# Weights and half of the data transposed by DMA in a fused S4 and linear attention kernel

## The chip, the cores and the metric

The kernel runs on one core of a Trainium2 chip. A core has five engines that run their own instruction queues: TensorE (PE; matmuls and transposes, with weight loads counted apart as PEld), VectorE (DVE), ScalarE (ACT), GpSimd (POOL) and SyncE (SP), which in this kernel issues nearly all DMAs. The metric is the device time of one execution in microseconds (us), as the median over runs; lower is better.

## The reference

Two layers read the same input x (2048 tokens x 512 channels, bf16) and are mixed by a gate of each token. Cut to what matters:

```python
g = sigmoid((x * gate_w).sum(-1, keepdims=True))
# A: a state space convolution of each channel d
K = einsum("dn,dnl,dn->dl", C, exp(dt * A * l), dt * B).real       # 512 x 2048 filter
y = irfft(rfft(pad(x)) * rfft(pad(K)))[:2048] + x * Dskip
# B: linear attention, 32 heads of 16
q, k, v = split(x @ wqkv)
phi(t) = concat([softmax(t @ w_phi), softmax(-(t @ w_phi))])
o = phi(q) @ (phi(k).T @ v) / (phi(q) . sum(phi(k)) + 1e-6)
out = g * y + (1 - g) * (o @ wo)
```

## The kernel before

**A plan with an order of its own.** The kernel does not emit instructions as it is read. Its functions register steps in a list (Plan.add, line 106; a DMA is registered by Plan.dma, line 127, as an issue, a transfer and a landing). Each step has an engine, or a choice of two; the steps it needs; and the rings (PSUM banks, buffers) it takes and drops. Plan.run (line 148) emits the steps in the order of the table ORDER, two characters a step, each pair a number in base 64 that counts in the list. For steps with two engines the string SIDES says which; for steps with two PSUM rings RINGS does; WARM puts up to six dummy matmuls ahead of a step (line 1560), FOURS says for each of the 16 filter units whether a product is summed by TensorE (four terms) or ahead of it by DVE (step A3, lines 1111 to 1115, then two terms), and ZPS says for each of the 8 key pairs whether the sums of the softmax are formed by TensorE first (lines 718 to 725). The costs that steps carry served to make these tables and have no part in the emitted program. Every engine, SP too, works through its own steps strictly in that order.

**The stages**, by the timeline of the profile:

1. To about 26 us: tables of sines (ACT) and index patterns, loads, and transposes. SP issues the q and k weights (load_wqk, line 1506, one DMA of 1 MB into wqk), small constants, the parameters of A, the input in 16 DMAs (load_ud, line 1495, tile UD, tokens on partitions), the v weights (load_wv). TensorE transposes two things. The input: eight steps xps (lines 493 to 506) of eight 128x128 transposes each, evicted into xT (step xT, channels on partitions; 16 blocks j of 128 tokens). The weights: fold (line 512), once for k and once for q, does two steps wtp of 16 transposes, evicted by two steps wTe into wT, and then two steps wps that multiply wT with the block matrix Wphi made from w_phi; their evictions wpe write the folded weights (WW[0:4] for k, Wqp for q). So the product with w_phi is folded into the projection.
2. From 26 to about 96 us: the keys (attention_keys, line 655) and the spectrum of the input (lines 566 to 641). For each of 8 key pairs s2 there are two products pk of a block of xT with WW, their exponentials ek (ACT, tile Ek), the sums zk (DVE, line 731 or 734), their reciprocals rz (ACT), two products vp for the values, evicted as vb, scaled by DVE (vr), and products kn that add to kvp. Every pk of a pair's first block waits for all of xT and all of the folded key weights (line 713: `[sp] + xt + kp`). Between them, for two halves of the channels, copies UDp of the input (step udc), products psAu evicted as XAu, and products psBu evicted as xst (step XU), which go to DRAM (XUd, step xuw). DVE and ACT also make the filter tables (p_ steps).
3. From 96 to about 225 us: for 16 units of 32 channels, filter products on DVE (A1, A2, A3, Rh, Rl, El), their sum over states on TensorE (kps), and transforms of the filter (psA, XA; psB, XK; product with XUX, step t128; psz, Zr; transposed through DRAM or by DVE; psy; step ou); beside them queries and attention outputs (plan_queries, line 809).
4. The tail: the last two units alone, and stores.

All evictions of PSUM go through one helper (Plan.copy, line 142), so the profile shows them under line 144 (ACT) and line 146 (DVE); the tile's name tells them apart. Exponentials and sines are line 68. The steps pzw and pzr (lines 343 to 356) write two small products of the parameters to DRAM and read them back as statE and statC in 8 DMAs each; statC is needed by the first sines of the units (tile cs).

Of the kernel before, what the change touches and what calls it, by code (L numbers as in the profile page):

```python
# [70 lines left out]
class Plan:  # L71

    DIGITS = "0123456789abcdefghijklmnopqrstuvwxyzABCDEFGHIJKLMNOPQRSTUVWXYZ-_"
    ORDER = ("0B0C0D0H0I0J2P000K0L0M112R2t2v0S0U0_100V120W0P0y0z0A2y2u0N0T14150O0Q0Y0X0Z18172Q2S2w2x0405060s0t0u0d0e0f0708090g0h0i0102030j"
             "0k0l0a0b0c0m0n0o0p0q0r0v0w0x130R2T2V2U2W2X2Z2Y2J2K192-0-1a1c1u2H1w1l162I1F2_311x1m1y1n1d1G1H3330322z2A341v2B2F2D1b2C352E1e1A"
             "1C2G1z361D2N2L2O37392M1o1p1q0E0F0G1r1s1t1B1E1W3a1J384A4H4J4I4K4W4Y4X4Z4O4L3b3d4S4M4P3e4N4T4Q4U1N3c513f554R4V3h4-3g563i4_5052"
             "5357595a5b5c5d3j5g1O3k543l585k5l5o5p5h3m5e5f1K5i4B5q4C5m5r5s3P5t3n5v5z3p5j5n3o5w5A1I1Q5u5D5E5F5G5H3u1L3q5x5B3w3x5K5O5y5C5S5L"
             "4D3v5P1R3r3s3t3y3z3A5T5I3Q3R5J5M5Q5U5Z1S5V1X1T1U1P3B3D3E615N5W625X5Y3C5R5-4E635_653I673K1M66683J3L3S6064696k6m3T3V6l6n6o6c6a"
             "6p3W3U6b6q6d3X3Z3Y6r3_3-1V1Z1Y406e1-1_25216s206t6v41433M3N3O3F3G3H1f1g1h426g45444647492627484a4b4c4d4e4g284f4h6h2b6i292a2d2c"
             "224i4j4k4l4n4o2e2m2f232g242h6w2i2j2n4m2o6f6j2q2p2r2k4s4t4p4q4r1i1j1k2l2s4u4v4w4x4y4z6E6G8j6x8x8y6u8i8n8k8m8o8l6y8p8q4F8u6z4G"  # L80
             "8z6D8v8w8A8B6F6H6I8D8E8R6K7b8C8F8J8K8G8H8I6J6L6M8S7c6N7d7f7haf6O8X8T7e7g6P6Q8Yag7i8L7K8-7M6R6S6T6U9c9d9e6V6W6X6Z6-6_8M8_7j8N"
             "7O8P7L8O7k8Q7N8U8V94907l957m7n8W8Z7Pao7Qap7oa5a9aa919293ah6Y707p7q7r6A6B6C9f9g9h9i9j9k7s7t7u7w7x7y9697a6a87173abadalamaq74ai"
             "aj72akauav98759a99a79bacae7RanaC777SaD9o7T789p76aras7vaE7U7VataI7Wawax9waL7A7C9x9q9y7XaM7D9r9z9s9AaJc6c77zaFaG9EbY7E7G7FaN7Y"
             "7Z7-7_80818384858r8s8t9B9C9D9t9u9v9l9m9nb0b1b2c09Fc17BaRaHc882869GaSb-c39M9NayaA87azaBaKb_7H88898b7Ic4aOaPaQ9Occcd8abZ8c7J8d"
             "aTc2c5aUcfcg8e79aVaW8f7a8gaXc9cachcbclcm8h9H9PcCaY9IcD9Qcectb9cubadZaZa-a_b6b7b89R9S9T9J9K9Ld-bhbicicjcEbbckcIcJbjd_e0cncobc"
             "bkbdbleMe1bpbxeN9-cvczcwcxcAe2bqbye3e4cQcRcSb3b4b59U9V9W9X9Y9ZbebfbgcyeOe5cpcrcqcse69_eVeWbra0dQcBa1a2dPdTdVdUcFcGa3bzeXcHeS"
             "a4cKbscLbte7e8e9bmbnboeaebeceeefegcTcUcVbubvbwcMcNcOcPdRbAd0d8bBbCbDbEcZc-c_d1d9ePeQeRedeTehd2daeUeidgdWejdhd3dod4dpdbdSdcdX"
             "dYcWcXcYe_f0eYeZdie-dqbFbGbHbIbJbKd5d6d7eGeHeIdddedfeAeBeCbLbMdjf1flbNdrdkfmdsdldmdnfGbOf2fHekbPf3f5eldCfofpfnfrfqfMbQfsfIfN"
             "bRf4f6ftf7fafuf8fvfJfKfLdtdudveDeEeFdwdxdydzdAdBdDdFdGfbfwdHdIf9fcfxfOfyeJeKeLemfPfQfzfRfSfTdEenfAfdfgfefffUeqfhfVfWfXfYfifZ"
             "f-eoerf_esepg0g1g2fBfjfCfDg3fkg4bSbTbUbVbWbXdMdNdOdJdKdLetexeyezeuevewfEfFg5g6g7g8g9ga")  # L90
    SIDES = ("01110001001011111100111001000001010101110000001110000000000011101000101111111100010100010000000000000000000000000000"
             "0000000000000000000000000010000000000000000001100001001")
    RINGS = ("00101010111010010100000000000000000000001010000000000000011001000010000000100110111010100010011111101100101101001111"
             "00100001")
    WARM = ("00000000000000610000000000002000060000000000000040000010000030000000000500050203000040000041500000000000100020000000"
             "00000000000002000000000")
# [97 lines left out]
def prepare(P, nc, g, evict, psum):  # L194

    fc, act, persist, at = g.fc, g.act, g.persist, g.at
    F = Bag()
# [19 lines left out]
    P.dma("wqk", 0.5, 2.0, lambda: g.load_wqk(), rw=("", "wqk"), move=3.3)  # L217
# [294 lines left out]
def fold(P, nc, g, evict, psum, first, dst, name):  # L512

    F, fn, out = Bag(), [], []
    for h in range(2):
        box = Bag()

        def fa(h=h, box=box):
            if h == 0:
                F.wT = g.up.tile([128, 4, 512], BF16, name=name, tag="wT")  # L520
            box.ps = psum([128, 4, 512], "wtp", BF16)
            for mm in range(2):
                for kt in range(4):
                    c0 = first + 128 * (2 * h + mm)
                    nc.tensor.transpose(out=box.ps[:, mm, 128 * kt:128 * kt + 128], in_=g.wqk[:, kt, c0:c0 + 128], identity=g.ident[:])

        def fe(h=h, box=box):
            i = box.ps[:, 0:2]
            box.ps = None
            return F.wT[:, 2 * h:2 * h + 2, :], i  # L530
        a = P.add("PE", "wtp", fa, [a] if h else [], take=[("ps", "p0")] + ([] if h else ["wT"]), rw=("wqk ic", ""))
        fn.append(evict("wTe", fe, [a]))
    for h in range(2):
        box = Bag()

        def fb(h=h, box=box):
            box.ps = psum([128, 2, 512], "wps")
            for k in range(2):
                for m in range(4):
                    kt = 2 * h + k  # L540
                    nc.tensor.matmul(box.ps[:, k, 128 * m:128 * m + 128], lhsT=F.wT[:, m, 128 * kt:128 * kt + 128], rhs=g.at.Wphi[:, m, :],
                                     start=True, stop=True)
# [12 lines left out]
def keys_and_spectrum(P, nc, g, psum):
# [8 lines left out]
    polar, sx, xt, kp = prepare(P, nc, g, evict, psum)  # L564
# [864 lines left out]
def full_kernel(tc, A_u, A_A_re, A_A_im, A_B_re, A_B_im, A_C_re, A_C_im, A_log_dt, A_Dskip,  # L1429
# [7 lines left out]
    with ExitStack() as ctx:  # L1437
        g, fc, at = Bag(), Bag(), Bag()
        P = Plan(nc, {"XAu": 1, "UDp": 1, "xst": 2, "wT": 1, "Ek": 2, "Zk": 2, "vr": 2, "vb": 2, "acc": 1, "r8": 3, "ax": 1, "nrm": 1, "E": 2, "cs": 4, "A": 1, "R": 2,
                      "KD": 1, "XA0": 1, "XK": 2, "Zr": 2, "XUX": 3, "ln": 8}, {"ps": 2, "p0": 2, "bk": 3, "acc": 1, "pf": 2})  # L1440
# [190 lines left out]
```

## Time and profile before

| | |
|---|---|
| median of 3 runs | 252.65 us (252.41 to 253.89) |
| the profiled execution | 252.06 us, span 250.3 us |
| mean granted TensorE clock | 0.957 |
| busy: PE, PEld, DVE, ACT, POOL | 206.6, 141.3, 234.2, 221.2, 8.7 us |
| HBM read and written | 21.38 MB, 12.58 MB |

The profile comes from one execution. An engine's busy time is the union of its instructions; neighbours overlap by a little under 0.1 us, so the durations of single instructions add up to slightly more. In a row of a timeline stand start and length in us, engine, line of the code, operation, the tile written and the tiles read; SPq and ACTq are the DMA issues in the queues of those engines. The span runs from the first to the last instruction, the profiled time also holds what lies around it.

### The profile page before, as it was taken

What the parts mean: (1) busy time and instruction counts of PE and PEld (TensorE: products, weight loads), DVE (VectorE), ACT (ScalarE), POOL (GpSimd) and SP (SyncE); (2) the same over time, 40 slices, a digit from 0 to 9 for tenths busy, and PEclk for the clock granted to TensorE, in tenths of its full rate; (3) what the DMA queues carried; (4) which work ended last, traced back from release to release, by engine and by line L of the source; (5) the groups of instructions that cost most, each with busy time, mean ns of one, the idle gap of its engine ahead of it and who ended that gap; (6) DMA issues with size and microseconds to landing.
All of it is one profiled execution on the core that took longest, in us unless ns stands there. A gap on an engine that the chain in (4) does not pass through costs nothing. (4 is left out here: it accounts for less than half of the span.)

```text
span 250.3 us, 9879 instructions
## 1 busy us (share of the span) xinstructions
PE 206.6 (83%) x4393; PEld 141.3 (56%) x4415; DVE 234.2 (94%) x318; ACT 221.2 (88%) x305; POOL 8.7 (3%) x21
## 2 busy tenths in 40 slices
PE   0675999999984685999988887999989789889960
PEld 0675656555754432365656645775678467777530
DVE  7999998899999999999999999999999999998880
ACT  3998998999999999999999999999999997892830
POOL 5700000000000000000000000000000000000000
PEclk9999999999997596899999999999999999999996
DMA  7997000080551755003787049723595989872934
GB/s 187 220 218 182 18 3 4 3 243 14 145 151 59 198 150 146 3 3 115 182 245 185 5 122 204 245 86 66 157 245 133 237 230 319 197 226 50 220 75 84
DMA packets 52842, 34.86 MB, mean 139 GB/s; under 512 B 30528, under 2 KB 48320, under 8 KB 52800
## 3 DMA queue, kind: packets, MB, share of 16 engines
q1 hardware_dynamic: 51744, 33.98, 53.4%
q8 instruction: 34, 0.56, 0.9%
q10 hardware_dynamic: 1056, 0.26, 0.5%
q14 instruction: 8, 0.07, 0.1%
HBM read 21.38 MB, written 12.58 MB: 136 GB/s over the span
## 5 line engine op out<-in xcount | busy, mean ns | idle before, releaser
L178 PE MATMUL kps<-R,A 128*32 128x64 bf16 x1600 | 29.1, 229 | 2.5 <-ACT XK L144 0.8
L178 PEld LDWEIGHTS <-A 128*32 128x32 bf16 x1600 | 27.2, 160 | 6.5 <-issue 3.0
L68 ACT ACTIVATE cs<-args 128x1024 bf16<-128x1024 f32 x32 | 30.6, 1050 | 0.0
L1102 DVE TENSOR_TENSOR A<-Ctab,Dtab 128x2048 bf16<-128x2048 bf16 x16 | 19.5, 1218 | 0.6 <-PE kps L178 0.6
L1123 DVE TENSOR_TENSOR R<-E,cs 128x2048 bf16<-128x2048 bf16 x16 | 19.5, 1218 | 0.0
L1107 DVE TENSOR_TENSOR A<-Ctab,Dtab 128x2048 bf16<-128x2048 bf16 x16 | 19.5, 1218 | 0.0
L1119 DVE TENSOR_TENSOR R<-E,cs 128x2048 bf16<-128x2048 bf16 x16 | 19.5, 1217 | 0.0
L144 ACT CAST XA<-psA 128x1024 bf16<-128x1024 f32 (+1 forms) x17 | 16.1, 986 | 2.5 <-PE psA L185 2.4
L144 ACT CAST Zr<-psz 128x1024 bf16<-128x1024 f32 (+1 forms) x16 | 15.8, 1025 | 2.0 <-DMA Zd<-Zr 1.6
L68 ACT ACTIVATE Ek<-pk 128x512 bf16<-128x512 f32 x32 | 16.6, 611 | 1.0 <-PE pk L704 1.0
L68 ACT ACTIVATE E<-args 128x1024 bf16<-128x1024 f32 x16 | 16.8, 1052 | 0.4 <-issue 0.2
L68 ACT ACTIVATE Eq<-pq 128x512 bf16<-128x512 f32 (+1 forms) x28 | 16.8, 688 | 0.3 <-PE pq L838 0.3
L1233 DVE TENSOR_TENSOR t<-XUX,XK 128x2048 bf16<-128x2048 bf16 x14 | 16.9, 1219 | 0.1
L144 ACT CAST XK<-psB 128x1024 bf16<-128x1024 f32 (+1 forms) x17 | 16.1, 981 | 0.6 <-DVE t L1233 0.6
L838 PE MATMUL pq<-xT,Wqp 128*128 128x512 bf16 x64 | 16.5, 395 | 0.1
L752 PE MATMUL vp<-WW,xT 128*128 128x512 bf16 x62 | 15.7, 380 | 0.1
L704 PE MATMUL pk<-WW,xT 128*128 128x512 bf16 x57 | 14.8, 380 | 0.5 <-issue 0.2
L611 PE MATMUL psB<-XAu,TB 64*128 64x128 bf16 x256 | 11.0, 241 | 3.8 <-ACT xst L144 2.6
L731 DVE TENSOR_REDUCE Zk<-Ek 128x64 f32<-128x1024 bf16 x12 | 14.0, 1210 | 0.0
L65 ACT ACT_TABLE_LOAD x10 | 12.8, 1283 | 0.9 <-PEq L1615 0.7
L611 PEld LDWEIGHTS <-TB 64*128 64x128 bf16 x256 | 9.0, 106 | 8.0 <-issue 7.9
L761 DVE TENSOR_TENSOR vr<-vb,vr 128x1024 bf16<-128x1024 bf16 x16 | 10.5, 683 | 1.7 <-ACT vr L68 1.5
(213 smaller groups left out, 506.4 us busy)
## 6 DMA issues: line engine op xcount, KB each, us to landing
XUX<-XUd SPq DMA_DIRECT2D x32, 256.0 KB, 4.9
XUd<-xst SPq DMA_DIRECT2D x8, 512.0 KB, 3.0
ax<-apd SPq DMA_DIRECT2D x16, 256.0 KB, 5.1
Zd<-Zr SPq DMA_DIRECT2D x24, 128.0 KB, 3.5
ZT<-Zd SPq DMA_DIRECT2D x6, 512.0 KB, 6.1
UD<-in_A_u_dram SPq DMA_DIRECT2D x16, 128.0 KB, 4.2
XUd<-xst SPq DMA_DIRECT2D x8, 256.0 KB, 4.0
wqk<-in_B_wqkv_dram SPq DMA_DIRECT2D x1, 1024.0 KB, 5.5
```

Of the source, the lines that this page charges most:

```text
L68: return self.nc.scalar.activation(**kw)
L144: self.nc.scalar.copy(out=o, in_=i)
L178: nc.tensor.matmul(kps[32 * dj:32 * dj + 32, g4, e, :], lhsT=A[:, ka, :, :, d].rearrange("p a b -> p (a b)"), rhs=R[:, kr, d, :], start=(i ...
L611: nc.tensor.matmul(box.ps[:, c2, sl, :], lhsT=fc.TB[rows, b0:b0 + 2].rearrange("p a b -> p (a b)"), rhs=X.t[rows, k, r0 + sl].rearrange("p ...
L704: nc.tensor.matmul(box.ps[:], lhsT=xT[:, st, kt, :], rhs=g.WW[:, kt, :], start=(kt == 0), stop=(kt == 3))
L752: nc.tensor.matmul(box.ps[:], lhsT=xT[:, st, kt, :], rhs=g.WW[:, 4 + kt, :], start=(kt == 0), stop=(kt == 3))
L838: nc.tensor.matmul(box.ps[:, m - m0, :] if late else box.ps[:], lhsT=g.Wqp[:, kt, 128 * m:128 * m + 128], rhs=xT[:, 4 * b:4 * b + 4, kt, : ...
L1102: nc.vector.tensor_tensor(out=c.A[:, 0:2].rearrange("p o a b c -> p (o a) b c"), in0=g.C[U // 8][:, 0:2, :, d0 % 256:d0 % 256 + 32].rearra ...
L1107: nc.vector.tensor_tensor(out=c.A[:, 2:4].rearrange("p o a b c -> p (o a) b c"), in0=g.C[U // 8][:, 1:3, :, d0 % 256:d0 % 256 + 32].rearra ...
L1119: nc.vector.tensor_tensor(out=c.R[:, :, :, 32:64], in0=t.E[:, 1].unsqueeze(1).to_broadcast([128, 2, 32, 32]), in1=t.cs[:], op=ALU.mult)
L1123: nc.vector.tensor_tensor(out=c.R[:, :, :, 0:32], in0=t.E[:, 0].unsqueeze(1).to_broadcast([128, 2, 32, 32]), in1=t.cs[:, ::-1, :, ::-1], o ...
L1233: nc.vector.tensor_tensor(out=box.t, in0=Ls[r0 // ns].X[:], in1=box.XK[:].unsqueeze(1).to_broadcast([128, 2, 1024]), op=ALU.mult)
```

## The change

- The one load of the q and k weights becomes two DMA transposes of 512 x 512 (k first in the list, then q) straight into wqT, which has the layout that wT had. fold loses its wtp and wTe steps, and each wps waits for its own half.
- Of the eight xps steps, the last four (T8 = 4 to 7, token blocks j = 8 to 15) with their evictions are replaced: for each of the 8 blocks, four DMA transposes of 32 tokens x 512 channels from the input in DRAM into xT. The input itself is still loaded whole, as the spectrum needs it.
- The first pk of pair s2 waits for the rows of pair s2 alone.
- ORDER, SIDES, RINGS, WARM, FOURS and ZPS are new; the list has 1046 steps where it had 1035.

```diff
-    FOURS = ("0111110101011000")
-    ZPS = ("00000101")
+    FOURS = ("0111110001011000")
+    ZPS = ("00000001")
...
-    P.dma("wqk", 0.5, 2.0, lambda: g.load_wqk(), rw=("", "wqk"), move=3.3)
+    for k in (1, 0):
+        P.dma("wqT", 0.5, 2.0, lambda k=k: g.load_wqk(k), rw=("", f"wqT{k}"), move=2.6)
...
+        if T8 in g.TURN:
+            xt.append([P.dma("xtr", 1.6, 2.0, lambda j=2 * T8 + k: g.turn_x(j), move=1.0, cnt=4) for k in range(2)])
+            continue
         a = P.add("PE", "xps", tx, take=[("ps", "p0")], rw=(f"ud{T8 // 2} ic", ""))
-        xt.append(evict("xT", xe, [a]))
-    kp = fold(P, nc, g, evict, psum, 512, lambda: g.WW[:, 0:4, :], "wT1")
-    g.Wqn = fold(P, nc, g, evict, psum, 0, lambda: g.Wqp[:], "wT2")
-    return polar, sx, xt, kp
+        xt.append([evict("xT", xe, [a])])
+    kp = fold(P, nc, g, evict, psum, 4, lambda: g.WW[:, 0:4, :])
+    g.Wqn = fold(P, nc, g, evict, psum, 0, lambda: g.Wqp[:])
+    return polar, sx, sum(xt, []), xt, kp
...
-        a = P.add("PE", "wtp", fa, [a] if h else [], take=[("ps", "p0")] + ([] if h else ["wT"]), rw=("wqk ic", ""))
-        fn.append(evict("wTe", fe, [a]))
...
-        a = P.add("PE", "wps", fb, fn + [a], take=[("ps", "p0")], drop=(["wT"] if h else []), rw=("Wphi", ""))
+        a = P.add("PE", "wps", fb, [a], take=[("ps", "p0")], rw=(f"Wphi wqT{first // 4}", ""))
...
-            a = P.add("PE", "pk", pk, [a] if u else [sp] + xt + kp, take=["bk"] + ([] if u else ["Ek", "Zk", "vr"]), rw=("TBn", ""))
+            a = P.add("PE", "pk", pk, [a] if u else [sp] + r["xs"][s2] + kp, take=["bk"] + ([] if u else ["Ek", "Zk", "vr"]), rw=("TBn", ""))
...
+        g.TURN = (4, 5, 6, 7,)
...
-        g.wqk = g.up.tile([128, 4, 1024], BF16, name="wqk")
+        g.wqT = g.up.tile([128, 8, 512], BF16, name="wqT")
...
-        def load_wqk():
-            nc.sync.dma_start(out=g.wqk[:], in_=B_wqkv[:, 0:1024].rearrange("(kt p) c -> p kt c", p=128))
+        def turn_x(j):
+            for c in range(4):
+                nc.sync.dma_start_transpose(out=xT[:, j, :, 32 * c:32 * c + 32], in_=x2d.rearrange("(q j c) d -> j c q d", q=32, j=16, c=4)[j, c])
+        g.turn_x = turn_x
+
+        def load_wqk(k):
+            nc.sync.dma_start_transpose(out=g.wqT[:, 4 * k:4 * k + 4], in_=B_wqkv[:, 512 * k:512 * k + 512])
```

In the new order SP issues, ahead of the keys: two parameters, a quarter of the input, a parameter, dt, the q weights, a parameter, the constants, the k weights, the transposes of block 8, a quarter of the input, two parameters, a quarter, the v weights, the last quarter, and the transposes of blocks 11 and 15, a store pzw, and those of 13, 9, 10, 12 and 14. Both reads pzr come behind the stores xuw of the spectrum's first half, that of statC behind one of the second half too.

More of the change, by code (lines that the diff above doesn't have):

```diff
@@ L73 @@
     DIGITS = "0123456789abcdefghijklmnopqrstuvwxyzABCDEFGHIJKLMNOPQRSTUVWXYZ-_"
[L74 to L96, printed above, removed]
@@ L97 @@
-    FOURS = ("0111110101011000")
-    ZPS = ("00000101")
+    ORDER = ("040506000K0L0M0O0P0N0V0X0Y0g0h0i0m0n0o2C2E0102030j0k0l2w0W2x120Q0Z0R130_2D0S140T1517180-101b0U1611193e1c1a0E0F0G0d0e0f1I0y0z"
+             "0A0B0C0D2K2L2M0p0q0r0708090a0b0c2y2z3a3c3b3d1z1e2B2A1d1o1p2F1f1q1J361x1A1B1K38371Q2I2J393f0s0t0u0H0I0J0v0w0x2T2U2V3334351r1s"
+             "1t2Z2-2_2N2O2P2Q2R2S2W2X2Y3031321g1h2G2H1y1F1D1C1G4L4S4U4T4V4W4X55575658594Z513g3h4-4Y4_52535c3i3k5g501M3j3l5h5d5a3m543n5b1Z"
+             "5e1E1H5i5k5m5l5n1N5r3o5s3p1U5v5o5f3q3s5j5p3r3t5w1V5q5t5x5z5B5A1L3u5C3w5u3x5G5K5y3v3y5D1P1W1S5H5E5F5L5I5M5O5Q5V3A5J5P5R5S5N1X"
+             "1O5W3B3z613F633H3-5T3G625U1R1T3I645X685Z3_5-69405_1-3C3D3E3J3K3L5Y4M4N3M65603O6c3N3P66676d416a6e6g6i6h3T3U6b3V6f6j6k6v6x4O3W"
+             "42446w6y6z6l436A456m6B1i1j1k3X3Y3Z3Q3R3S4647484a496n4c1Y1_4b6r20286s6o2123226p4d6t4e4f4g4h6C4i4k6q6G2a2c4j29242e6H6D4p4l4r4q"
+             "2b2d254s2f2g6E2i2p2h1l1m1n4m4n4o1u1v1w4t4u4v4w4y4x4z4A4B4C2q2r4D4F6u4G262j4P2k2l6I272m2t2s2n2u2o2v8t8x4E8v8z8u6F6J8y8w8A8B4H"
+             "4I4J4K8I8J6K6O8K6P8F6R4Q4R6T8O8G8H8L8M6Q6S8P907m6V8N8Q8U8R8S8T8V6U916W7n7o6Xaq6Y7q7s6Z967r7t6-ar8W8X7p926_977V997X8Y706L6M6N"
+             "9t9u9v9q9r9s9n9o9p71727374757678797a9a8Z7W7u7Z8-7v7-8_93949bas9f7w9g957x7y98az7_7Y7zaAagakal9c9daB777baw9eax9haham9i7c7A7B7C"
+             "7D7E7F7H7I7Jajaoat7dau7GaFaGav7K7e7f9j7g9l9kai7i9manapayaNaO809z819A7L9HaCaDaPaT8283aE7M7h9I847j9BaU859JaHaI7NaWchaXci9C9K86"
+             "9D9L9w9x9y8788899M9N9O8a8b8c8e8f8g9Pc77Pcbccb0aQaR9QaSaY9Rb17O9X9Yc9cecj8d9Z8hb8b9ba9E9F9Gbbbcbdbhbibj8C8D8E7RaJaLaKcaaM7Scf"
+             "7Q8i8jaVc87T8k8maZa-a_8nb2ckclcd8lcg8o8pcq8qcrb38r7k7lcscmcncocwcxb4b6b57U8s9S9-cNb79TcO9_bkcpcEblcFe8bseae9btctcucKcGbmcLcv"
+             "bu9U9V9Wa0a1a2a3a4a5d5d6d7bebfbga6a7a8ebcyczbnbvbobwecbAf4edcHcIcTeef5efbBcPegcUcJa9bIehbJaaeXeYabbxbybzeiejekbpbqbrcAcCcBcD"
+             "cMd_acadd-bCcQeZcRaeafcSbKe2e4e3bDbEc_d0d1elemenepeqercVcWbLbMf1f2e0cXcYcZc-dbdje5dcdkbFbGbHd2d3d4bNbObPe-e_faf0eoesdddlf3dr"
+             "dzdsdedmdAe1dfdnbQbRbSd8d9dabTbUbVdgdhdieReSeTdodpdqe6e7f7f6f8dtf9fbbWdufwbXdBfxbYfcdCdvfddDfzfAfyfBfCfDfRfefgetfSbZb-fhffeu"
+             "evfifEewfXb_fUfVfTfWfYdNeLeMeNeOePeQdwdxdydEdFdGdHdIdJdKdLdMfFc0fjfGfldOfHfmdQdRdSfkdPfndTfIfZeUeVeWc4c5c6dXdYdZc1c2c3exf-f_"
+             "g0g1g2fJfKfofrfpg3eyezfLfqfseBfMg4g5g6g7eCeDeEftfNg8g9fufOgagbdUdVdWeAeFeGeHeIeJeKgcgdfPfvfQgegfgjgkglggghgi")
@@ new lines @@
+    SIDES = ("01111101000001000000110110100010000010111000000000000010000101110111100000100000100000000000010001000000000000000010"
+             "00000000000000000011000101000000000100000000001")
+    RINGS = ("00110011010000000000000000000000101000000000000000100100100000000010111101011111101000111110101001011010110110000001")
+    WARM = ("00000000000201010150000000001160110000000004000002000020000246000000014400043000000001000000001000000000000001310020"
+             "00000100000000000000000")
@@ L504, in xe, with fold @@
             return g.xT[:, 2 * T8:2 * T8 + 2].rearrange("p j k s -> p (j k s)"), i.rearrange("p j k c q -> p (j k c q)")
+        if T8 in g.TURN:
+            xt.append([P.dma("xtr", 1.6, 2.0, lambda j=2 * T8 + k: g.turn_x(j), move=1.0, cnt=4) for k in range(2)])
+            continue
         a = P.add("PE", "xps", tx, take=[("ps", "p0")], rw=(f"ud{T8 // 2} ic", ""))
-        xt.append(evict("xT", xe, [a]))
-    kp = fold(P, nc, g, evict, psum, 512, lambda: g.WW[:, 0:4, :], "wT1")
-    g.Wqn = fold(P, nc, g, evict, psum, 0, lambda: g.Wqp[:], "wT2")
-    return polar, sx, xt, kp
[L512 to L530, printed above, removed]
-        a = P.add("PE", "wtp", fa, [a] if h else [], take=[("ps", "p0")] + ([] if h else ["wT"]), rw=("wqk ic", ""))
-        fn.append(evict("wTe", fe, [a]))
+        xt.append([evict("xT", xe, [a])])
+    kp = fold(P, nc, g, evict, psum, 4, lambda: g.WW[:, 0:4, :])
+    g.Wqn = fold(P, nc, g, evict, psum, 0, lambda: g.Wqp[:])
+    return polar, sx, sum(xt, []), xt, kp
+def fold(P, nc, g, evict, psum, first, dst):
+    out, a = [], None
     for h in range(2):
@@ L540, in fb @@
                     kt = 2 * h + k
-                    nc.tensor.matmul(box.ps[:, k, 128 * m:128 * m + 128], lhsT=F.wT[:, m, 128 * kt:128 * kt + 128], rhs=g.at.Wphi[:, m, :],
+                    nc.tensor.matmul(box.ps[:, k, 128 * m:128 * m + 128], lhsT=g.wqT[:, first + m, 128 * kt:128 * kt + 128], rhs=g.at.Wphi[:, m, :],
                                      start=True, stop=True)
-            if h == 1:
-                F.wT = None
         def fg(h=h, box=box):
@@ L563, in evict @@
         return P.add(("ACT", "DVE"), name, lambda: P.copy(*get()), deps, drop=["psum"], **kw)
-    polar, sx, xt, kp = prepare(P, nc, g, evict, psum)
+    polar, sx, xt, xs, kp = prepare(P, nc, g, evict, psum)
     g.XUn = {}
@@ L643, in shift @@
     def shift():
-        g.UD = g.wqk = None
+        g.UD = g.wqT = None
         g.shift()
@@ L651, in keys_and_spectrum @@
     sp = P.add("X", "x_psum", shift_psum, [n for n in P.nodes if n.psum is not None and not isinstance(n.psum.take[0], str)], take=["acc"], opens="bk")
-    return dict(polar=polar, xt=xt, kp=kp, sh=sh, sp=sp, bank=bank, evict=evict)
+    return dict(polar=polar, xs=xs, xt=xt, kp=kp, sh=sh, sp=sp, bank=bank, evict=evict)
 def attention_keys(P, nc, g, psum, r):
@@ L1438, in full_kernel @@
         g, fc, at = Bag(), Bag(), Bag()
-        P = Plan(nc, {"XAu": 1, "UDp": 1, "xst": 2, "wT": 1, "Ek": 2, "Zk": 2, "vr": 2, "vb": 2, "acc": 1, "r8": 3, "ax": 1, "nrm": 1, "E": 2, "cs": 4, "A": 1, "R": 2,
+        P = Plan(nc, {"XAu": 1, "UDp": 1, "xst": 2, "Ek": 2, "Zk": 2, "vr": 2, "vb": 2, "acc": 1, "r8": 3, "ax": 1, "nrm": 1, "E": 2, "cs": 4, "A": 1, "R": 2,
                       "KD": 1, "XA0": 1, "XK": 2, "Zr": 2, "XUX": 3, "ln": 8}, {"ps": 2, "p0": 2, "bk": 3, "acc": 1, "pf": 2})
```

## Prediction

> **What bounds the kernel now.** I read the page's totals first, then a table of busy time by stage, then the timelines of VectorE (DVE) and ScalarE (ACT), and last the DMA issues.
>
> ```profile
> span 250.3 us, 9879 instructions
> PE 206.6 (83%) x4393; PEld 141.3 (56%) x4415; DVE 234.2 (94%) x318; ACT 221.2 (88%) x305; POOL 8.7 (3%) x21
> ```
>
> The profiled execution took 252.06 us; its span is 250.3, with 1.8 us around it. The median of the three runs shown is 252.65, 0.6 above the profiled one. DVE is the busiest engine, but a share of 94% says nothing of where the other 6% lie. The next view gives busy time by stage (columns: stage and length, then PE, weight loads, DVE, ACT, POOL, granted clock, DMA share, GB/s):
>
> ```profile
> 5.00:25.00 20.00, 13.01 (x150) 12.09 (x151) 19.78 (x35) 18.53 (x24) 4.96 (x9) 1.00 1.07 207
> 25.00:75.00 50.00, 48.48 (x782) 29.69 (x789) 46.87 (x68) 47.75 (x87) 0.00 (x0) 1.00 0.25 73
> 75.00:210.00 135.00, 115.52 (x2674) 78.23 (x2684) 133.41 (x163) 132.18 (x167) 0.00 (x0) 0.94 0.56 148
> 210.00:245.00 35.00, 29.63 (x792) 21.31 (x794) 30.42 (x35) 21.45 (x29) 0.00 (x0) 1.00 0.66 166
> ```
> ```profile
> 240.78 2.43 DVE L1373 TENSOR_TENSOR xT<-psy,gT 128x1024 bf16<-128x1024 f32 x3
> ```
>
> From 5 to 210 us DVE idles 0.2, 3.1 and 1.6 us, and ACT 1.5, 2.2 and 2.8: both engines run almost without gaps, so work has to leave both. Only after 210 has ACT room. DVE's last instruction ends at 243.2; its first starts at 1.2. Between these 242.0 us lie 234.15 busy and 7.9 idle: 0.3 early, 3.1 from 25 to 75, 1.6 to 210, 2.8 in the tail. The rest of the span is the last stores. So the time is DVE's work plus DVE's waits, and I forecast the two apart.
>
> **The change, in DVE and ACT work.** The order table holds two digits for each planned step (a number in base 64), the sides table one bit for each step that may go to either engine. Reading both by the list of steps, before and after, shows which evictions vanish and which change engine. Their prices (columns: count, then shortest/median/longest ns, first and last start), first DVE's evictions, then ACT's:
>
> ```profile
> L146 DVE CAST vb<-vp x11: 680/684/692, 31.6 to 87.9; 128x512 bf16<-128x512 f32 x11
> L146 DVE COPY UDp<-UD x5: 416/420/421, 24.7 to 64.5; 128x1024 bf16<-128x1024 bf16 x5
> L146 DVE CAST XAu<-psA x5: 1215/1215/1224, 28.3 to 71.1; 128x1024 bf16<-128x1024 f32 x5
> L146 DVE CAST xst<-psB x5: 1214/1218/1225, 48.0 to 63.4; 128x1024 bf16<-128x1024 f32 x5
> L146 DVE COPY wT<-wtp x4: 675/677/682, 8.5 to 14.4; 128x1024 bf16<-128x1024 bf16 x4
> ...
> L146 DVE COPY xT<-xps x2: 681/681/681, 23.5 to 25.6; 128x1024 bf16<-128x1024 bf16 x2
> ```
> ```profile
> L144 ACT CAST XAu<-psA x11: 987/1022/1072, 26.5 to 74.6; 128x1024 bf16<-128x1024 f32 x11
> L144 ACT CAST xst<-psB x11: 993/1020/1053, 45.5 to 91.2; 128x1024 bf16<-128x1024 f32 x11
> ...
> L144 ACT COPY xT<-xps x6: 1001/1012/1025, 14.3 to 25.1; 128x1024 bf16<-128x1024 bf16 x6
> L144 ACT CAST vb<-vp x5: 585/592/624, 35.4 to 52.9; 128x512 bf16<-128x512 f32 x5
> ...
> L144 ACT COPY UDp<-UD x3: 1047/1048/1053, 16.7 to 23.2; 128x1024 bf16<-128x1024 bf16 x3
> ```
> ```profile
> L731 DVE TENSOR_REDUCE Zk<-Ek x12: 1208/1210/1216, 29.4 to 66.0; 128x64 f32<-128x1024 bf16 x12
> ...
> L734 DVE TENSOR_REDUCE Zk<-zk x2: 691/692/693, 59.5 to 67.4; 128x128 f32<-128x512 f32 x2
> ```
> ```profile
> L1112 DVE TENSOR_TENSOR A<-A 128x2048 bf16<-128x2048 bf16 x7 | 8.5, 1218 | 0.0
> ```
>
> Up to the first filter product, DVE: the four weight evictions go (4 x 0.68 = -2.7); data evictions go from 2 to 3 (+0.7); folded weights 2 to 0 (xst's shape, -2.4); UDp copies 5 to 7 (+0.8); XAu 5 to 7 (+2.4); xst 5 to 3 (-2.4); values (vb) 11 to 8 (-2.1). ZPS loses a one, so one pair of key tiles is summed by two 1.21 reductions, not by TensorE and one of 0.69 (+1.7). Sum -4.0. Behind that: oT 5 to 3 (vb's shape, -1.4); XK 0 to 2 (no row on DVE; at xst's 1.22 for the same shape +2.4, bounds 1.2 to 2.7 for both, from a bf16 1024 copy's 0.68 to XAu's longest); FOURS loses a one, so unit 7 gets its A3 product back (+1.2); small moves of the tail (Y, bsg, KD, Zr) come to about +0.5 at the 0.68 of 512 elements. Sum +2.7, and DVE's whole work changes by **-1.3 us**. The point between the two sums is this row:
>
> ```profile
> 96.12 1.22 DVE L1102 TENSOR_TENSOR A<-Ctab,Dtab 128x2048 bf16<-128x2048 bf16 x1
> ```
>
> ACT to the same point: xT 6 to 1 (-5.1), folded weights 2 to 4 (XAu's shape, +2.0), UDp 3 to 1 (-2.1), XAu 11 to 9 (-2.0), xst 11 to 13 (+2.0), vb 5 to 8 (+1.8): -3.3; behind it oT 7 to 9 (+1.2), XK 17 to 15 (xst's shape, -2.0), small moves about -0.5 (0.59 for each 512 elements): -1.3. In all **-4.6 us**. Where it lands matters: the early relief is larger, as p_fc, the last two p_t and an XAu also move behind the first key reduction (2 x 0.68, 0.9 and 1.2 of DVE). Before that reduction DVE has 7.9 less and ACT, before its first Ek, 6.1 less.
>
> ```profile
> 27.39 3.07 ACT L68 ACTIVATE Ek<-pk 128x512 bf16<-128x512 f32 x6
> ```
> ```profile
> 27.45 0.89 DVE L412 TENSOR_SCALAR pb<-pt 128x256 int32<-128x256 f32 x4
> 28.25 1.22 DVE L146 CAST XAu<-psA 128x1024 bf16<-128x1024 f32 x1
> 29.39 2.33 DVE L731 TENSOR_REDUCE Zk<-Ek 128x64 f32<-128x1024 bf16 x2
> ```
>
> So the first Ek can come at 27.4 - 6.1 = 21.3 us, and the reduction 2.0 us behind it at 23.3, while DVE would be there at 21.5: **1.8 us of new DVE waiting**. From there to the first filter product DVE has 3.9 us more than before.
>
> TensorE loses 64 transposes (32 of weights, 32 of data), the 8 sums of one key pair and half of unit 7's products, and gains 9 dummy matmuls. The 17% of the span in which it idles cover both, so I cost it at nothing; without that cover it would be a gain, since far more products go than come. Two output stores (four issues) move from SP's queue to ACT's in the tail: 2.4 us at SP's 0.61 for an issue (below), under the 13.5 us of room that ACT has there; nothing, and at worst 1.2 if an eviction stands right behind one.
>
> **The transposes.** No DMA transpose is in this trace, so its cost is bounded by the nearest rows:
>
> ```profile
> WW<-in_B_wqkv_dram SPq DMA_DIRECT2D x1, 512.0 KB, 3.8
> ...
> statC<-pz SPq DMA_DIRECT2D x8, 32.0 KB, 2.6
> ```
> ```profile
> 10.31 7.26 SPq L1497 DMA_DIRECT2D UD<-in_A_u_dram  x12
> ...
> 21.95 3.71 SPq L354 DMA_DIRECT2D statC<-pz  x8
> 49.24 18.63 SPq L623 DMA_DIRECT2D XUd<-xst  x8
> ```
>
> A weight is 512 KB: at least 3.8 us to landing like WW, at most 16 blocks of 32 KB one after another at 2.6, 42 us. I take 4 to 5, by WW, the row of the same bytes. Issue slots on SP are 0.46 to 0.61 us (8 in 3.71, 12 in 7.26). The second weight, the 14th issue, goes out at about 9 us and lands at 14.
>
> ```profile
> 16.45 1.10 PE L541 MATMUL wps<-Wphi,wT 128*128 128x128 bf16 x16
> ```
>
> Its fold takes 1.1 us, and ACT, four evictions before its first Ek at 21.3, wants it at about 17: some 2 us are spare. I add 0.7 us of waiting for it and for the small constants, which are issued later than now (0 to 2). The order of SP gets 33 more issues, 32 for data: 15 to 20 us. They fill the hole between 25.7 and 49.2, and the 8 reads of statC (3.7 us) move out of it, far back. The last transpose then lands near 44 us.
>
> ```profile
> 49.45 2.04 ACT L68 ACTIVATE Ek<-pk 128x512 bf16<-128x512 f32 x4
> ```
> ```profile
> 92.19 7.44 ACT L68 ACTIVATE cs<-args 128x1024 bf16<-128x1024 f32 x8
> ```
>
> Pair 4, the first that waits for such rows, has its Ek at 49.45 now and 4 us earlier then, and its two transposes are not the last of the row. If they were late, its products would hold the value, key-value and spectrum products behind them on TensorE, and ACT its Ek. Behind the transposes on SP stand the XUd stores; the cover fails if an issue takes over about 0.8 us. The moved reads of statC come behind a store of the second half and end, by a rough estimate, when ACT comes to the sines (92.19 less its 3.3): up to 2 us of ACT waiting, in the range and not in the sum.
>
> [...]
>
> **Sum.** DVE work -1.3. Waits: +1.8 before the first reduction, +0.7 for weights; from 25 to 75 both engines have more to do inside the stage, so I take half of its 3.1 away (-1.5); in the tail ACT's work has become DVE's, so 1.0 of its 2.8 go. Net waits 0. 252.06 - 1.3 = 250.8 against the profiled run, 251.4 on the scale of the median. I forecast **251.1 us**; its own range, with each wait term free by its own size, is 249 to 253.
>
> **Rivals.**
> A. *The early lead is kept.* Both engines start the keys 6 us early; if the order fills the waits, DVE keeps the 4.0 us it saves up to the first filter product and pays back only half of the 2.7 behind it, as 2.8 us of tail waits can absorb it. For: ACT loses 4.6 us where both engines are full. Against: DVE, not ACT, ends last. Time: 252.06 - 4.0 + 1.3 = 249.4, and with 25-75 free of waits 247.
> B. *The weights come late* (slower). Place: the key fold; it decides once the second weight lands after about 16 us. At 10 us each, one behind the other from 6.2, they land at 26; two folds and evictions put the first Ek at 30, 2.6 later than before. DVE then has 3.9 more before the filter, minus 2.9 us of waits it can fill, and 1.7 more behind it: +5.3, **257 us**. For: the DMA share is 1.07 from 5 to 25 us, so the queues are already full. Against: the WW row.
> C. *Blocks go one by one.* At the 42 us above, the second weight lands at 90, the keys start 65 us late: 315 us. [...] Against: 32 KB take 2.6 us and 512 KB only 3.8, so most of a small transfer's time is fixed and overlaps with its neighbours.
> D. *The new order meshes worse* in 75-210, where DVE waits only 1.6 us: if both engines wait there as they do from 25 to 75 (3.1 in 50 us), that is 8.4, +6.8 less 1.3: 257.5; half of that gives 255.
>
> **Chances.** Forecast 0.47, A 0.31, B 0.10, C 0.03, D 0.09. About 1% (2.5 us) is what a measurement of this kernel tells from no change, so faster means under 250.1 and slower over 255.2. Faster: A and a little of the forecast, 0.33. Same: 0.46. Slower: B, C and most of D, 0.21. The range, 247.4 to 256.0, leaves out C, the outer half of B and D, and the end of A.
>
> **What would show it.** Right: first Ek at 21 to 24 us; no eviction of wT; DVE busy 232 to 234 us; both weights landing in under 6 us; transposes issued at under 0.7 us each; first A product 1 to 3 us before 96.1. Wrong: TensorE waiting for the weights past 16 us; a key product waiting for xT; XUd stores starting after 52 us; DVE idle of over 10 us between first and last instruction.

## The result and the profile after

The changed kernel takes **270.86 us** (median of 4 runs, 268.46 to 272.18) beside 253.27 (252.41 to 254.10, 4 runs) for the kernel before on the same chip: a ratio of 1.068, 95% interval 1.060 to 1.077. That is 17.6 us slower; the forecast was 251.1, its range ended at 256.0. In some of the experiments a few executions came out over 1.5% longer than the shortest of the same kernel: the medians and ranges below hold all executions, the ratios leave those out. The profiled execution of the changed kernel took 272.18 us. Its page, totals and the chain that ended last:

```profile
span 270.4 us, 9663 instructions
...
PE 210.3 (78%) x4264; PEld 140.8 (52%) x4289; DVE 233.3 (86%) x314; ACT 218.1 (81%) x303; POOL 8.9 (3%) x21
...
SPq 28%; PE 23%; ACT 19%; DMA 11%; DVE 10%; issue 6%; DVEq 0%; ACTq 0%
```

DVE has 0.9 us less to do than before and ACT 3.1 less; all of the loss is waiting, and the largest share of the chain is SP's queue, an engine that has no computing instruction in this kernel. By stage (PE, weight loads, DVE, ACT, POOL, clock, DMA share, GB/s):

```profile
5.00:25.00 20.00, 9.64 (x80) 8.79 (x81) 14.41 (x27) 14.68 (x20) 5.18 (x9) 0.95 0.70 142
25.00:75.00 50.00, 40.51 (x626) 24.00 (x631) 36.73 (x52) 35.51 (x65) 0.00 (x0) 0.92 0.34 83
75.00:210.00 135.00, 112.26 (x2351) 73.07 (x2359) 127.98 (x163) 127.55 (x171) 0.00 (x0) 0.92 0.48 133
```

DVE idles 5.6, 13.3 and 7.0 us in the three stages, where it idled 0.2, 3.1 and 1.6. The first product of the filter is the same mark as in the prediction (96.12 us there):

```profile
109.77 1.22 DVE L1085 TENSOR_TENSOR A<-Ctab,Dtab 128x2048 bf16<-128x2048 bf16 x1
```

So 13.7 us are lost up to it, and 6.4 behind it (270.4 - 109.8 = 160.6, before 250.3 - 96.1 = 154.2). What SP did meanwhile, from its timeline (start, length of the group, line, operation, target and source, count):

```profile
5.22 3.33 SPq L1496 DMA_TRANSPOSE wqT<-in_B_wqkv_dram  x1
...
10.78 2.37 SPq L1496 DMA_TRANSPOSE wqT<-in_B_wqkv_dram  x1
13.20 5.08 SPq L1492 DMA_TRANSPOSE xT<-in_A_u_dram  x4
18.32 2.18 SPq L1481 DMA_DIRECT2D UD<-in_A_u_dram  x4
...
27.09 12.40 SPq L1492 DMA_TRANSPOSE xT<-in_A_u_dram  x8
39.61 0.98 SPq L345 DMA_DIRECT2D pz<-pt  x2
40.64 27.46 SPq L1492 DMA_TRANSPOSE xT<-in_A_u_dram  x20
68.21 3.37 SPq L606 DMA_DIRECT2D XUd<-xst  x4
```

The 32 data transposes hold the queue for 5.08 + 12.40 + 27.46 = 44.9 us. What stands behind them is late: behind the weights and the first four, the second quarter of UD at 18.3 us (10.3 before); behind the next eight, the store of pz at 39.6 (18.8); behind the last twenty, the first XUd store at 68.2 (49.2). The view of one line's instructions (shortest/median/longest ns, first and last start; then the time from issue to landing) gives the price of one:

```profile
L1492 SPq DMA_TRANSPOSE xT<-in_A_u_dram x32: 1166/1237/2477, 13.2 to 66.9; - x32
...
DMA to landing us min/median/max: 2.3/2.4/4.7
```
```profile
L1496 SPq DMA_TRANSPOSE wqT<-in_B_wqkv_dram x2: 2370/2848/3326, 5.2 to 10.8; - x2
...
DMA to landing us min/median/max: 4.5/4.9/5.3
```

Landing is quick, 2.4 us for 32 KB and 4.9 for 512 KB. Issuing is not: 1.24 us and 2.85 in the median. A few issues are longer, up to 2.5 us, so that the 32 take 44.9 us, 1.40 each, and not 32 x 1.24 = 39.7. Who waited for what, ACT and then DVE (total us, times, longest):

```profile
ACT xst L143 <- DMA XUd<-xst: 9.0, 2, 7.1
ACT Ek L68 <- PE pk L687: 4.1, 3, 2.4
```
```profile
DVE gz L652 <- PE gps L648: 3.7, 1, 3.7
DVE vb L145 <- PE vp L735: 3.1, 3, 1.7
DVE pt L377 <- DMA pz<-pt: 2.9, 1, 2.9
DVE xT L145 <- PE xps L499: 2.8, 1, 2.8
```

The longest is ACT's: it may not write the next spectrum tile into xst, a ring of two, until the late stores have read the old ones. The others are the same queue seen from other engines: gps waits for the last rows of xT, pt for the late store of pz, xps for the late quarter of UD.

### The profile page after: what moved, and what is told of

It reads as the page before. It is cut to its first block, busy times and chain, and to the rows that moved or that the text cites. A ratio compares the mean times of both kernels' runs of the same rounds, so it can differ in the third digit from the quotient of the medians.

```text
span 270.4 us, 9663 instructions
## 1 busy us (share of the span) xinstructions
PE 210.3 (78%) x4264; PEld 140.8 (52%) x4289; DVE 233.3 (86%) x314; ACT 218.1 (81%) x303; POOL 8.9 (3%) x21
## 4 chain that ended last, share of the span: by engine, by line
SPq 28%; PE 23%; ACT 19%; DMA 11%; DVE 10%; issue 6%; DVEq 0%; ACTq 0%
SPq L1492 16%; DMA XUd<-xst 5%; ACT cs L68 4%; SPq L1481 3%; PE pq L821 3%; PE kps L177 3%; DMA ax<-apd 3%; DMA Zd<-Zr 2%; ACT Eq L68 2%; ACT xst L143 2%; SPq L1496 2%; PE psy L802 2%; PE psA L184 2%; ACT E L68 2%; SPq L354 2%
## 5 line engine op out<-in xcount | busy, mean ns | idle before, releaser
L177 PE MATMUL kps<-R,A 128*32 128x64 bf16 x1536 | 27.9, 229 | 2.8 <-DVE A L1095 2.5
L177 PEld LDWEIGHTS <-A 128*32 128x32 bf16 x1536 | 26.1, 160 | 6.8 <-DVE A L1095 2.8
L143 ACT CAST xst<-psB 128x1024 bf16<-128x1024 f32 x13 | 13.0, 1025 | 9.1 <-DMA XUd<-xst 9.0
L821 PE MATMUL pq<-xT,Wqp 128*128 128x512 bf16 x64 | 17.4, 406 | 0.1
L714 DVE TENSOR_REDUCE Zk<-Ek 128x64 f32<-128x1024 bf16 x14 | 16.4, 1210 | 0.0
L143 ACT CAST XK<-psB 128x1024 bf16<-128x1024 f32 (+1 forms) x15 | 14.3, 974 | 1.0 <-DVE t L1216 0.8
L1245 PE MATMUL psz<-t,TI 128*128 128x512 bf16 x40 | 11.6, 379 | 3.0 <-ACT XA L143 0.7
L1002 PE MATMUL args<-selE,statC 64*128 64x512 bf16 x32 | 7.3, 433 | 8.3 <-ACT cs L68 4.3
## 6 DMA issues: line engine op xcount, KB each, us to landing
XUX<-XUd SPq DMA_DIRECT2D x32, 256.0 KB, 5.4
ax<-apd SPq DMA_DIRECT2D x16, 256.0 KB, 4.5
XUd<-xst SPq DMA_DIRECT2D x8, 256.0 KB, 4.9
```

What stands on the lines that cost most here:

```text
L143: self.nc.scalar.copy(out=o, in_=i)
L177: nc.tensor.matmul(kps[32 * dj:32 * dj + 32, g4, e, :], lhsT=A[:, ka, :, :, d].rearrange("p a b -> p (a b)"), rhs=R[:, kr, d, :], start=(i ...
L714: nc.vector.tensor_reduce(out=K.Z[:, u].rearrange("p g h -> p (g h)"), in_=K.E[:, u].rearrange("p g (h f) -> p (g h) f", f=16), axis=mybir ...
L821: nc.tensor.matmul(box.ps[:, m - m0, :] if late else box.ps[:], lhsT=g.Wqp[:, kt, 128 * m:128 * m + 128], rhs=xT[:, 4 * b:4 * b + 4, kt, : ...
```

## The experiments

**Transposes replaced by ordinary DMAs.** The same 32 rows, the same place on SP, the same bytes, but not transposed, so that the second half of xT holds untransposed rows; in the second kernel the weights too are loaded without being transposed.

```diff
-    nc.sync.dma_start_transpose(out=xT[:, j, :, 32 * c:32 * c + 32], in_=...[j, c])
+    nc.sync.dma_start(out=xT[32 * c:32 * c + 32, j].rearrange("p k s -> p (k s)"), in_=...[j, c])
```

> The changed kernel, but each of the 32 data transposes is an ordinary DMA of the same 32 rows, 32 KB, at the same place of the SP queue (the rows land untransposed in the second half of xT, so the outputs are others). Theory: the loss comes from SP, which needs 1.2 to 1.4 us to issue a transpose of this size against some 0.5 us for an ordinary DMA; then the 32 issues take about 16 us and not 45, the first store of XUd goes out before 50 us and not at 68, and the time falls from 271 to 254 to 259. Rival 1, the number of issues in the queue is what costs, whatever their kind: it stays above 264. Rival 2, the new order itself meshes worse: it stays above 264 with XUd stored early.

> As the run with ordinary loads for the data, and the two weight transposes are ordinary DMAs of 512 KB too (wrong layout, same bytes, other outputs). Theory: SP gains another 4.8 us ahead of the second quarter of the input, so the second pair of input transposes on TensorE starts near 19 us and not at 23.4, and the first Ek at 22 to 25; the time is 2 to 5 us below the run with ordinary data loads, 251 to 256. Rival 2, the order: still above 262. If the weights cost nothing, it is within 1 us of the run with ordinary data loads.

Measured: 254.98 us (251.94 to 258.59), ratio to before 1.005 (1.000 to 1.009), and with plain weights 253.91 (251.77 to 255.80), 1.004 (0.999 to 1.008); before took 252.85 in these runs. By the ratio the first is some 1.2 us over before, where the changed kernel was 17.6: almost the whole loss is gone. The two ratios are 0.3 us apart, which the intervals do not tell from nothing. So the second is not 2 to 5 us below the first: of its cases, the one in which the weights cost nothing came true, although its first Ek comes 2.2 us earlier (23.9, in the first 26.1). SP in the second:

```profile
28.14 10.13 SPq L1492 DMA_DIRECT2D xT<-in_A_u_dram  x20
51.53 4.94 SPq L606 DMA_DIRECT2D XUd<-xst  x4
```

Twenty issues take 10.1 us, 0.51 each, in place of 27.5: the same twenty cost the queue 2.7 times as much as transposes. The XUd stores come 16.7 us sooner. And with loads at the ordinary price, the whole of the rest of the change gains nothing: 253.9 against 252.85.

**The price put into the kernel before.** 26 transposes of the same shape into unused bytes, in SP's hole; no instruction waits for their data.

```diff
+            for i in range(26 if qi else 0):
+                nc.sync.dma_start_transpose(out=to[i // 8][...], in_=g.x2d.rearrange("(q j c) d -> j c q d", q=32, j=16, c=4)[8 + i // 4, i % 4])
```

> The kernel before, with 26 transposes of 32 rows of the input into unused bytes added to the SP queue behind the reads of statC, that is in its hole from 25.7 to 49.2 us; nothing waits for their data. Theory: they hold SP until about 25.7 + 26 x 1.3 = 60 us, the first XUd store is 10 us late, ACT and DVE wait for the xst buffers, and the time rises by 4 to 10 us, to 257 to 263. Rivals (late data of the transposes, or the new order): no change, 252 to 254.

Measured: 264.27 us (262.73 to 265.89), ratio 1.046 (1.038 to 1.054), a little over the expected range. Its SP queue and the wait that follows:

```profile
26.02 11.07 SPq L358 DMA_TRANSPOSE TF<-in_A_u_dram  x8
...
61.10 2.52 SPq L358 DMA_TRANSPOSE idle<-in_A_u_dram  x2
63.73 17.10 SPq L627 DMA_DIRECT2D XUd<-xst  x8
```
```profile
DVE xst L146 <- DMA XUd<-xst: 11.1, 1, 11.1
```

The issues last from 26.0 to 63.6 (1.45 us each), the stores start 14.5 us late, and one wait of DVE for xst is 11.1 us; the time rises by 11.4. Order, engines and the work of all others are untouched and nothing waits for the data, so transposes in the queue suffice for such a loss. That it is their issue and not their transfer follows from the next experiment, which moves the same bytes.

**What in a transpose costs: rows or the instruction.** One transpose of 128 neighbouring rows for each block in place of four of 32; the bytes are the same, the tokens are others, and so the keys computed from them.

```diff
-            for c in range(4):
-                nc.sync.dma_start_transpose(out=xT[:, j, :, 32 * c:32 * c + 32], in_=...[j, c])
+            nc.sync.dma_start_transpose(out=xT[:, j], in_=x2d[128 * j:128 * j + 128, :])
```

> The changed kernel with one transpose of 128 neighbouring rows per block in place of four of 32: 8 issues in place of 32, the same bytes. It reads other tokens than the reference wants, so the computed keys are others. If the price of a transpose is per instruction (about 1.2 us each): some 10 to 12 us of SP in place of 45, XUd stores before 58 us, and 254 to 258 us in all. If it is per row or per byte: SP is busy with them for about 40 us as before and the time stays at 266 to 272 us. In between, by the two sizes already seen (1.24 us for 32 rows, 2.8 us for 512 rows: about 1.1 us and 3.4 ns per row), 1.5 us each and 12 us in all.

Measured: 254.00 us (252.17 to 258.35), ratio 1.001 (0.997 to 1.005).

```profile
L1491 SPq DMA_TRANSPOSE xT<-in_A_u_dram x8: 1257/1267/2639, 13.3 to 34.3; - x8
...
DMA to landing us min/median/max: 2.7/2.9/5.0
```

1.27 us for 128 rows beside 1.24 for 32 in the median, with the longest at 2.6 and 2.5: up to there the price is that of the instruction. The same bytes in a quarter of the issues lose nothing: the ratio leaves 0.2 us. (A block of the kernel takes four sets of 32 rows, each with a step of 64 tokens, so this form cannot serve it.)

**Half as many, and the stores first.** In one kernel only T8 = 6 and 7 are turned by DMA (16 transposes), T8 = 4 and 5 again by TensorE ahead of the keys (ORDER and the other tables follow). In the other all 32 stay, but the last 8 stand behind the first four XUd stores.

```diff
-        g.TURN = (4, 5, 6, 7,)
+        g.TURN = (6, 7,)
```

> The changed kernel with a quarter of the data turned by DMA instead of half: 16 transposes of 32 rows instead of 32, the other quarter by TensorE ahead of the first key. By the issue price (1.24 us each) SP is busy with them for 20 us instead of 40, from about 24 to 45 us, and the XUd stores start at 52 to 56 us, undelayed: 254 to 259 us. If the time fell only in proportion to the number of transposes, or if the new order with data by TensorE is what costs (263 us with none turned by DMA): 262 us or more.

> The changed kernel with its last 8 transposes behind the first two pairs of XUd stores on SP instead of ahead of them; nothing is taken away. If only the place in the queue is at fault: xst comes free some 8 to 10 us earlier and the time is 258 to 264 us. If SP's sum of issue time is at fault (72 us of issues in the first 81 us): the last key pairs wait for their rows instead, and the time stays at 264 to 271 us.

Measured: 256.34 us (255.54 to 256.80), ratio 1.013 (1.009 to 1.018), and 277.80 (276.76 to 280.64), 1.100 (1.094 to 1.106). With 16:

```profile
22.53 6.52 SPq L1494 DMA_TRANSPOSE xT<-in_A_u_dram  x4
29.17 1.11 SPq L347 DMA_DIRECT2D pz<-pt  x2
30.33 16.74 SPq L1494 DMA_TRANSPOSE xT<-in_A_u_dram  x12
53.38 4.91 SPq L608 DMA_DIRECT2D XUd<-xst  x4
```

They end at 47.1, ahead of the stores, and of the 17.6 us over before 3.6 are left: 16 fit into the hole, 32 do not. The other kernel came out worse than either theory had it. xst's stores are earlier, but the rows are later, and TensorE's gate product waits for them with DVE behind it:

```profile
PE gps L650 <- DMA xT<-in_A_u_dram: 11.1, 2, 6.4
```
```profile
DVE gz L654 <- PE gps L650: 11.3, 1, 11.3
```

Both places that were tried for the 45 us of issues lose, the stores' waits in one and the rows' in the other. That fits a sum that is too large for this stretch of SP; other places, or another engine's queue for the data, were not tried.

**The order without the transposes.** The kernel before up to the first filter product, and from there the changed kernel's order, engines, rings and dummy products.

> The kernel before up to its first filter product (order, engines, rings, no DMA transposes), and behind that the new order, engines, rings, dummies and unit 7's A3 product. Between the first filter product and the end the changed kernel needs 160.6 us, the one before 154.2. If this part of the loss belongs to the new order, this kernel takes 256 to 260; if it only follows from the late start and its queues, 251 to 254.

Measured: 255.67 us (254.80 to 256.70), ratio 1.012 (1.006 to 1.019), between the two expectations. Behind the front of before, the later order costs 2.8 us. Some 2 us of it are work and not waiting: DVE is busy 236.2 us here, 234.2 before. The prediction has this work, as the +2.7 behind the first filter product; the -4.0 ahead of it, which pays for it in the changed kernel, is missing here. The rest is waiting. The stage from 75 to 210 us has 5.2 us of DVE idle, 1.6 in the kernel before:

```profile
75.00:210.00 135.00, 111.74 (x2526) 73.17 (x2538) 129.84 (x159) 127.19 (x162) 0.00 (x0) 0.94 0.51 137
```

**Data by TensorE, weights by DMA, and combinations.** Five kernels looked for a version that keeps a part of the change. The first is the changed kernel with `g.TURN = ()`. The next three are the kernel before with only the weights turned by DMA, in the last of them with the keys' half on ScalarE's queue. The fifth joins the front of the kernel with 16 transposes to the later order of before.

> The changed kernel with its second half of the data again turned by TensorE (four more psum transposes and evictions, put into the new order ahead of the keys) and only the weights turned by DMA. Theory (the issue time of the 32 data transposes on SP is the loss): the XUd stores start before 55 us again, the waits for xst go, and the time is 253 to 257 us, like that of the kernel in which the 32 rows came by ordinary DMAs. Rival (the new order itself, or the two weight transposes, cost most of it): 262 us or more.

Measured: 263.30 us (261.79 to 265.27), ratio 1.039 (1.032 to 1.046): a miss on the rival's side. ACT's waits for xst fall from 9.0 to 1.3 us, but all eight xps steps now stand ahead of the first key, and the order loads the last quarter of UD late, behind the weights and wv:

```profile
PE xps L501 <- DMA UD<-in_A_u_dram: 9.1, 2, 6.9
```

Its first Ek starts at 30.7 us (27.4 in the kernel before). That part is again a late issue on SP. The first filter product is 8.0 us late (104.1), and the first XUd store is at 58.5 with SP's queue empty since 24.4; what makes up the rest was not tried. The kernel does not tell order and queue apart.

> The kernel before, with only the weights turned by DMA transposes: its own order, engines and rings, less the four wtp and wTe steps; SP issues the small weights, the keys' transpose, then the data as before, with the queries' transpose ahead of the last quarter of the data. VectorE is rid of 2.6 us of evictions, SP gets 5 us of issues more in its first 20 us. If VectorE's work decides: 250 to 251.5 us. If SP's queue in the front decides (the last quarter of the data lands 4 us later and the first key product waits for it): 252 to 254 us, no gain.

> The same as the one before it, with three copies of the data (UDp from UD) moved from ScalarE (1.05 us each) to VectorE (0.42 us each): ScalarE is rid of 3.2 us ahead of its first exponential. If the engines' work ahead of the first key decides: 249.5 to 251 us and the first Ek ahead of 26.5 us. If the landing of the last quarter of the data decides: as the one before it, 252 to 254 us.

Measured: 261.44 us (259.71 to 262.92), ratio 1.031 (1.026 to 1.036), and 261.26 (259.41 to 262.10), 1.031 (1.026 to 1.036), both far above what was expected. The queries' half was issued at 16.0 us, and its products stand in TensorE's order ahead of the polar tables (psri of C):

```profile
21.12 1.89 PE L528 MATMUL wps<-Wphi,wqT 128*128 128x128 bf16 x16 [2.69 <-DMA wqT<-in_B_wqkv_dram]
```

The wait is 2.7 us on PE, the psri products come 4.3 us later than before, and the first Ek 4.5 us later (31.9). The 2.6 us of evictions taken from DVE gain nothing beside that.

> The kernel before with only the weights turned by DMA, placed anew: the keys' half is issued on ScalarE's queue, in the time in which that engine has nothing to do (2.0 to 5.4 us), the queries' half on SP between the first and the second of the last three quarters of the data, and its products on TensorE stand behind the first data blocks and not ahead of the polar tables; two copies of the data go from ScalarE to VectorE. Theory (a transpose costs its issue time on the queue that issues it, and nothing where that queue is idle): first Ek at 26 to 27.5 us and a total of 250 to 252.5 us, 9 to 11 us below the kernel that issued both on SP. Rival (weights turned by DMA cost the time by themselves, wherever they are issued): 258 us or more.

Measured: 257.72 us (255.77 to 258.58), ratio 1.018 (1.014 to 1.023): 3.7 us better than with both on SP, but neither the 250 to 252.5 expected nor the rival's 258. The first Ek is at 27.6 us and the first filter product at 96.4, as in the kernel before. What it loses comes later, with the later order of before unchanged; a part of it is told in the last section.

For the fifth, "the one before it" is the kernel with 16 transposes.

> The one before it up to the first filter product, and from there on the order, engines, rings and filling products of the kernel before. From the kernel with the front of before and the later order of after (2.8 us over before) the later order of before should be worth 2 to 3 us: 251 to 256 us. If the two halves must be timed to each other (the later order fits only the front for which it was made): 257 us or more.

Measured: 261.21 us (259.05 to 264.73), ratio 1.034 (1.028 to 1.039). Its first Ek is early (24.7), its first filter product is not (97.4). Each half does better with the half that it was made for (256.34 and 252.74 us), so the joint has a cost of its own, a part of which the last section shows. No version found beats the kernel before.

## Why the prediction was wrong

**The failed step** is the price of an issue: "Issue slots on SP are 0.46 to 0.61 us", taken from ordinary DMAs and given to the transposes, so that 33 more came to 15 to 20 us. Ordinary DMAs do cost that here (0.51 each for the twenty of the first experiment). A transpose of 32 rows costs 1.24 in the median and 1.40 in the mean, one of the weights 2.4 to 3.3. The prediction bounded the transfer from both sides (3.8 to 42 us) and did not bound the issue, though it named the point at which its cover fails, "if an issue takes over about 0.8 us". The hole from 25.7 to 49.2 us has room for 32 issues of 0.73 us; 16 that take 23.3 us in all fit (256.3 us), 32 that take 44.9 do not (270.9).

The transfer is near that of an ordinary DMA: 2.4 us to landing for 32 KB and 4.9 for 512 KB, where the same 32 rows as ordinary DMAs took 1.9, and the v weights, an ordinary DMA of 512 KB in the changed kernel, 5.0. The time in the queue that issues is not: the same twenty issues took 27.46 us as transposes and 10.13 as ordinary DMAs, 2.7 times.

**The early front.** Forecast: first Ek at 21.3 us. It came at 27.7. With all loads plain it comes at 23.9, so the engines' relief was real and 2.6 us of it were over-estimated; the other 3.8 are issue time ahead of UD's quarters, 2.2 of the weights and 1.6 of the first data blocks (26.1 with the data alone plain). The forecast sized the weights' wait at 0.7 us: wps waited 0.5 for them.

**The weights** landed in 4.5 to 5.3 us, as assumed (4 to 5). Rivals B and C fall by that: a weight does not take C's 42 us, and the weight fold was not what started the keys late. That the weights gain nothing either was not foreseen.

**The work** was right in DVE: 233.3 busy (forecast 232 to 234, -1.3, measured -0.9). ACT fell by 3.1, not by 4.6.

**The other waits** were put at nothing in sum (+1.8, +0.7, -1.5 and -1.0). The kernel with all loads plain shows them with issues at the ordinary price. Its span, 252.0, is 1.7 us over before: DVE is busy 0.8 less (233.4) and idle 3.8 more between its first and last instruction, and what follows DVE takes 1.3 less. By stage its idle time changes by +2.7 from 5 to 25 us (forecast +2.5), -1.1 from 25 to 75 (-1.5), +2.8 from 75 to 210 (no term) and -0.5 in the tail (-1.0). So the terms of the sum came out within 0.5 us, and the stage that has none, from 75 to 210 us, took 2.8:

```profile
75.00:210.00 135.00, 111.72 (x2546) 73.03 (x2553) 130.56 (x160) 127.88 (x163) 0.00 (x0) 0.94 0.53 143
```

DVE idles 4.4 us there, 1.6 in the kernel before. Rival D, at 0.09, named this stage and was right in kind; it said 6.8 us, or half of that. An earlier front (first filter product at 95.1, before 96.1) and these waits leave 253.9: no gain, no clear loss.

Of the four signs set down as "wrong" three came true: XUd stores after 52 us (68.2), a key product waiting for xT (3.1 us), DVE idle over 10 us (25.9 from 5 to 210); TensorE waiting for the weights past 16 us did not. Of the signs set down as "right", the weights' landing, the missing evictions of wT and DVE's work held; the issues under 0.7 us, the first Ek and the first filter product (13.7 us late) failed. Two slips in the prediction's sums decide nothing: rival A's 249.4 less 3.1 is 246.3 and not 247, and the second weight is the 15th issue on SP, not the 14th.

What stays open: which step of the later order makes DVE wait longer from 75 to 210 us. It is not the front: behind the front of before the same order idles DVE 5.2 us there.

## What to carry to other kernels

Price a DMA twice, its transfer and the time it holds the queue that issues it, and bound the second as carefully as the first: an operation without a row may transfer like its neighbours and still cost the queue 2.7 times as much, as the transposes of 32 rows did here. Add up the issues between the neighbours that must stay on time, and divide the hole by the count; that threshold decided here. Where transposes by DMA are wanted, few large ones may cost the queue less than many small ones: here 8 issues of 128 rows held it for 12.8 us in place of the 44.9 of 32 issues of 32 rows, and the loss was gone.

## What the hardware showed that was not expected

The issue price of a transpose is nearly flat from 32 to 128 rows of 512 bf16 elements (medians of 1.24 and 1.27 us) and 2.3 to 3.5 us for 512 rows on SP; one of 512 rows, issued first of all on ACT's queue, took 1.42. The runs do not show why.

In the four kernels that join the later order of before to another front, TensorE stops for 1.9 to 2.4 us in the middle of one group of kps products, near 140 us, with nothing that it waits for in the trace; the kernel before and the changed one have no such stop over 1 us. In the kernel with the keys' weights on ACT's queue the clock falls behind it, to 0.50 in one stretch of 2 us; its TensorE rows and then its stages of 2 us:

```profile
133.02 2.02 PE L179 MATMUL kps<-R,A 128*32 128x64 bf16 x115 [0.69 <-ACT XA L145]
136.94 0.45 PE L179 MATMUL kps<-R,A 128*32 128x64 bf16 x13 [1.91 <-issue]
```
```profile
136.00:138.00 2.00, 1.06 (x16) 0.55 (x17) 0.57 (x1) 1.22 (x4) 0.00 (x0) 0.76 0.08 28
138.00:140.00 2.00, 2.00 (x40) 1.31 (x42) 2.00 (x3) 1.00 (x1) 0.00 (x0) 0.50 0.04 8
```

115 of the 128 products run, then 13 after the stop; the granted clock is 0.76 and 0.50 from 136 to 140 us, and DVE and ACT stand for 1.4 and 1.8 of these 4 us. DVE waits 1.9 us in all for these products, of the 3.7 us by which this execution (255.77 us, the shortest of six) has a longer span than the one before.

The traces point to the loading of TensorE's program, though no run was made to test it. The profile lists a DMA queue of its own for instructions:

```profile
q8 instruction: 34, 0.56, 1.0%
```

Its 34 packets carry 16 KB each, and TensorE runs 8792 recorded instructions in this kernel, some 259 a packet. In each of the four kernels the fifteenth packet starts only 0.3 to 0.6 us before the stop, 9.5 to 9.9 us behind the fourteenth, and TensorE stops behind its record 4021 or 4033 (the first two of the four have some 20 records fewer). Two of them have a second stop over 1 us near 198 us, with the twenty-fifth packet just ahead of it: behind record 6593, which is ten packets and 2560 records later, 256 a packet. In the ten other kernels the fifteenth packet has landed at least 36 records before record 4033, and none has such a stop. So TensorE seems to have run out of instructions; why the packet comes so late in these four is open.
